# A new step order, key features on GpSimd, and wide products over all heads in an attention and FFN kernel on one core

## The chip, the cores and the metric

The kernel runs on one NeuronCore of a Trainium2 chip. The metric is the device time of one execution in microseconds, from the first to the last instruction with what lies around them; the median of three runs is given. Five engines work side by side, each through its own queue in order: TensorE (PE in the profile, its weight loads PEld), VectorE (DVE), ScalarE (ACT), GpSimd (POOL) and SyncE (SP), which issues most of the DMAs. They wait for each other by semaphores alone.

## The reference

Two blocks follow each other. The first is an attention without softmax: queries and keys are sketched to 8 + 8 numbers, whose outer product is a feature vector of 64.

```
def phi(x):                                  # q, k, v: (4, 4, 1088, 32); S1, S2: (8, 32)
    a = np.einsum('rd,bhsd->bhsr', S1, x)
    b = np.einsum('rd,bhsd->bhsr', S2, x)
    return np.einsum('bhsi,bhsj->bhsij', a, b).reshape(*x.shape[:-1], r * r)
q_p, k_p = (phi(q), phi(k))
kv = np.einsum('bhsf,bhsd->bhfd', k_p, v)
z = np.sum(k_p, axis=2)
num = np.einsum('bhsf,bhfd->bhsd', q_p, kv)
den = np.einsum('bhsf,bhf->bhs', q_p, z)[..., None] + 1e-06
attn = num / den
```

Its output, reshaped to 4352 rows of 128, goes through a multiplicative FFN:

```
a = x @ w1; b = x @ w2                       # 128 x 1024 each
h = a * b @ w3                               # 1024 x 1024
return h @ w_out                             # 1024 x 128
```

S1, S2 and the four FFN matrices are float64 and reach the core as raw 64-bit words.

## The kernel before

**Steps and order.** The kernel is a dictionary of small named steps, each a Python function that issues a few instructions. A string, ORDER, names all of them once; the steps are run in that order, and every engine's instructions are chained in it (lines 1514 to 1527). So ORDER is the queue of every engine at once, written out by hand or by a planner, and an instruction that waits holds up everything behind it on its own engine. Three more tables go with it: SLOTS gives each tile its buffer (`b` are the 8 PSUM banks, `x` three large buffers that k, v and q share, `raw` three for weight words), POOL names the steps that run on GpSimd instead of VectorE, ACTS those on ScalarE. `on(name)` looks a step up there.

**Steps by their names.**

- `s.*` prepares the sketches S1 and S2 from their words and spreads them into block tables (`s.blk`, `s.blkh`, `s.KS`, `s.AR`, `s.RC`), and their products for the denominator (`s.P*`).
- `k0` to `k3` are the keys of a batch: `load`, `max`, `g`, `lead` and `rest` split k into two parts; `gram` forms k's Gram matrix on PE; `Gm` to `Nr` turn it, in small VectorE steps with a few products between them (`T0`, `T1`, `N0`, `N1`), into a vector for the denominator; `tr`, `kT`, `ab`, `abc` or `abt` make the sketches of k, `kp` their outer products (the features), `kv` the product of features and v. `kr0`, `kr1` do the last 64 rows of two batches each. `kz`, `kq` are the transposed results that the queries are multiplied with.
- `q0` and `q1` are the two halves of batch 0's first 1024 queries, `q2` and `q3` those of batch 1, `q4` and `q6` the 1024 of batches 2 and 3 ("wide"), `qr` the last 64 rows of all four batches. `tr`, `max`, `l2`, `l1`, `rm` split them; `A*` and `C*` are their products with the sketches (L957, L1278, L1287); `sm` to `sc` put leading and remaining parts together; `al`, `p01`, `p2`, `p12`, `dn`, `de`, `rc` give the denominator and its reciprocal; `phi` is the outer product of features (L1128, L1382), `pt`/`pc` or `pT` its transposition, `x` the product with kz or kq (L1188, L1401), `xT` the copy into the FFN's input.
- `w0` to `w10` load and convert the weights: `c` and `m` on ScalarE, `j` on VectorE, `a0`, `a1` on GpSimd (L438). `f0` to `f7` multiply w3 and w_out into one matrix, w3o.
- `g0` to `g7` are the FFN for 512 rows each, `gr` for the last 256: for each of 8 chunks `a` and `b` on PE (L1441, L1451), `c` the copy of a to SBUF on ScalarE (L1446), `m` the product a times b on VectorE (L1457), `o` the product with w3o (L1464, L1471), then `oT` and `st` for the output.
- `warm` steps are products of zeros whose result nobody reads (L221).

Every float32 product on PE appears as two matmul rows in the trace. In `q_part` the first rows, q0, are of kind "A", the branch `if cut:`, with one multiply `xs`, one set of transposes `xt` and one copy `xT` for all 512 columns. In `q_wide` the last products `x` run in one or two parts `u`, with the row strip t outside and the heads h inside, and `A0` adds onto what the bank's start by `C0` left.

Of the kernel before, what the change touches and what calls it, by code (L numbers as in the profile page):

```python
# [61 lines left out]
c.zeros c.mask c.ident warm17 s.four k0.zero k0.loadr warm0 k0.load0 k0.load1 k0.max0 k0.max1 k0.g k0.lead0 s.load  # L62
k0.rest0 s.words warm3 k0.tr0 warm19 warm1 k0.gram0 k0.gram1 k0.lead1 k1.zero warm4 warm14 k0.tr1 s.pair s.low s.lead
s.sum s.rest s.T s.tc s.P q0.load k0.rest1 s.zero s.R k0.kT1 k0.gram2 q0.tr k0.gram3 k1.load q1.tr k1.loadr kr0.load
s.c q0.max k0.gram4 w1.load s.blk k1.max q0.l2 s.Pc k0.kT0 kr0.tr k0.ab1 k0.ab0 k0.Gm s.Pm s.blkh k0.Gt k1.g k0.Ga
q0.l1 q1.max k0.T0 k0.abc1 k0.Gb k0.T1 q1.l2 warm2 k0.kp1 warm21 warm7 k1.tr1 kr0.kT k0.abc0 k1.lead0 k0.Ta warm18
q0.A0 q1.l1 warm13 k0.kp0 warm28 k0.Tb kr0.ab kr0.abc k1.tr0 q0.rm s.Pp v0.zero k0.Ts k0.N0 k1.kT0 q0.C0 k1.rest0
v0.load q0.sma k0.N1 q0.sta k0.kv0 kr0.kp k0.kv3 v0.loadr k0.kv1 k0.kv2 k0.kvr k1.gram0 k1.gram1 k0.Na s.KS q0.sha
k0.Nr q0.C0t q0.sla k0.kvc k0.kvm warm5 warm12 q0.sca k0.Nf k0.Nb k1.kT1 k0.kzt k0.Nh k2.zero kr1.load kr1.tr q0.al
q0.phi0 q1.rm w0.load q0.A1 warm11 warm24 q1.A0 warm23 k0.kz kr1.kT kr1.ab warm16 k0.kqt warm22 warm6 k0.Nl q0.smy  # L70
q1.sm w1.c q0.sty k2.loadr q1.st q1.sh w0.c q0.pt0 warm10 q0.C1 q0.pc0 q0.shy k1.gram2 k1.gram3 q0.phi1 k1.gram4
q0.pt1 q0.C1t q0.pc1 w0.m q0.x0 q0.x1 q0.sly q0.p01 q0.scy q0.p2 q0.p12 q0.dn k1.Gm q0.de q0.rc w2.load q1.load q1.C0
w0.j q0.xs w0.a0 q1.sl k1.Gt q0.xt q1.scy q1.sca k1.Ga q1.p01 q1.al q0.xT q1.p2 q1.p12 k1.ab warm9 k1.abt q3.tr q1.dn
g0.3a q1.de w0.a1 w1.m w1.j g0.0a w1.a0 g0.2a q1.rc q1.bs q2.tr q1.phi g0.1a g0.2b g0.3c w2.m g0.3b w2.c k0.kq g0.0c
g0.4a k2.load k2.max q1.pt1 kr1.abc q2.max g0.4c g0.1c g0.3m q3.max q1.pt0 q1.pc0 q0.restT g0.6a g0.0b k2.g k1.Gb
k2.lead0 q1.pc1 w3.load k1.T0 q1.x k1.T1 k2.rest0 w2.j k1.Ta q2.l2 q1.xT k2.gram0 q1.restT k2.gram1 k2.gram2 k1.Tb
k1.Ts k2.gram3 k2.gram4 k1.N0 s.AR k1.N1 warm15 g0.0m k1.Na k1.Nb w4.load g0.2c q2.l1 w1.a1 g0.2m q2.load g0.4b g1.3a
k2.Gm g1.6a g0.6c w3.c k1.Nr g0.1b w4.m w3.j k2.Gt q2.rm g1.3c k2.Ga g1.5a g1.1a g1.6c w3.m k3.zero k2.Gb g0.1m g0.4m
s.RC g1.5c g1.1c q2.C0 q2.A0 q2.C1 k2.T0 k2.T1 v1.zero w2.a0 warm26 q3.l2 w4.c k3.loadr w3.a1 w3.a0 q2.At w2.a1 q2.Ct
q2.sm q2.st g1.5b q2.sh w4.j g1.1b g1.2b g1.0b g1.2a g0.6b g0.7b f0.t g1.2c g1.1m k2.Ta q2.sl w4.a0 q2.sc g1.5m f0.m  # L80
g1.4a g1.3b v1.loadr g0.6m w4.a1 g1.0a q2.p01 q2.al q2.p2 q2.p12 k2.Tb k1.kp0 k1.kp1 q3.l1 q4.tr g1.2m f1.t g1.4c
g1.0c g0.7a g0.5a f1.m q4.max g1.0m w5.load q2.dn w6.load w6.c q2.de v1.load k1.kv0 k1.kv2 k1.kv3 k1.kv1 k1.kvr q2.rc
w6.j q3.rm f0.o g0.7c g0.5c k1.kvc f1.o q3.C0 q3.A0 q3.C1 w6.m w9.load kh2.load warm20 k2.Ts g1.3m g0.0o g1.7b q2.bs
g0.7m k1.kqt g1.6b q3.At w9.m k1.kq w5.c g0.1o w7.load q2.phi0 w5.m q3.sm q3.Ct q2.pT0 g1.6m k2.N0 k2.N1 q3.st k2.Na
q2.x0 k2.Nb k2.kT1 g1.7a g0.5b w5.j w6.a1 w6.a0 q3.sh q2.xT0 g2.1a g1.7c w9.c g1.7m f3.t g0.5m w5.a1 v2.zero w5.a0
g2.6a q2.restT w9.j q3.sl q3.sc g2.0a w8.load g2.7a q4.l2 g1.4b f3.m g2.0c g2.1c w7.c w7.m f2.t k2.kT0 g1.4m q3.al
g2.3a g2.6b w9.a1 k2.Nr w9.a0 g2.0b f6.t f6.m q3.p01 q3.p2 w7.j q3.p12 g2.0m q3.dn f2.m q4.l1 f3.o w8.m g2.6c q3.de
g2.6m q4.rm k2.ab w8.c g2.7c f6.o g2.3c q4.C0 q4.A0 w8.j w7.a0 k2.abt w8.a1 q4.C1 warm8 f2.o g2.2a g0.2o g2.5a q4.Ct
g2.4a g2.7b w8.a0 w7.a1 g2.2c g1.0o f5.t q4.At k3.load kh3.load w10.load q3.rc q3.bs g2.4c g0.6o g1.1o q3.phi0 f5.m
f5.o w10.m g2.5c w10.c f4.t k3.max g2.7m k3.kT1 q3.pT0 f4.m g1.6o g1.3o q3.x0 f4.o q3.xT0 q4.sm g1.4o k3.g q4.st g0.3o  # L90
g0.5o q3.load g0.4o g3.1a g2.1b k2.kp0 kr1.kp k3.lead0 q4.sh v2.load q4.sl q4.sc w10.j g3.1c w10.a1 q4.al g1.5o q4.p01
w10.a0 f7.t f7.m g2.2b q4.p2 g2.5b q4.p12 q4.dn q4.de v2.loadr g2.1m q6.tr k2.kp1 q4.rc k3.kT0 k3.rest0 g3.6a g3.6b
g1.2o g3.6c f7.o g3.3a g0.7o g1.7o k2.kv0 k2.kv3 g2.5m g2.2m g1.oT k2.kv1 k3.ab k3.gram0 k3.gram1 k3.gram2 k2.kv2
k2.kvr k3.gram3 k3.gram4 q4.bs k2.kvc g3.3c warm27 g3.2a g3.2c q6.max k3.Gm g3.6m k3.Gt k3.Ga q3.restT g3.2b qr.max
v3.zero g2.4b g3.3b g3.0a q4.phi0 k3.Gb g0.oT g0.st v3.load k3.abt g3.4a q6.l2 k3.kp0 q4.phi1 q6.l1 g3.4c g3.4b q6.rm
g2.4m g2.3b q4.pT0 g3.3m q4.pT1 g3.0b g3.7a g2.0o k2.kqt g2.4o g3.7c k2.kq qr.l2 g3.2m g3.0c g2.6o g2.5o g2.3m g3.0m
k3.kp1 k3.T0 k3.T1 k3.Ta k3.Tb k3.Ts q4.x0 q4.x1 k3.N0 k3.N1 k3.kv0 k3.kv1 k3.kv3 v3.loadr k3.kv2 k3.kvr q4.xT0 q4.xT1
k3.Na k3.Nr g3.4m k3.Nb g3.5a q6.C0 q6.A0 q6.C1 k3.kvc k3.kqt k3.kq qr.l1 g3.5c g5.6a q6.Ct g3.7b q6.At q6.sm q6.st
q6.sh g5.0a g5.4a g5.4c g5.0c g5.2a g5.1a g2.3o q6.sl q6.sc q6.al q6.p01 q6.p2 q6.p12 q6.dn q6.de q6.rc q6.bs g5.5a
g2.2o g4.7a g5.5c g5.6c g5.1c g5.2c g5.7a g5.3a g3.1b g2.1o g5.3b g2.7o g3.0o g3.4o g5.7c q6.phi0 g5.3c q6.phi1 g3.1m  # L100
q6.pT0 g5.3m g2.oT q6.pT1 g3.3o q6.x0 q6.x1 g3.5b q6.xT0 q6.xT1 g3.1o g6.3a g6.1a g4.7c g5.6b g4.5a g6.3c g5.6m g4.5c
qr.rm g3.5m g3.7m g6.4a g3.6o g6.5a g5.1b g7.4a g6.5c g6.1c g6.4c g7.4c qr.C0 qr.A0 qr.C1 qr.Ct qr.At g4.0a g4.2a
g5.5b qr.sm g3.2o g5.0b g6.1b g4.4a qr.st qr.sh qr.sl qr.sc g4.0c g4.4c qr.al g6.1m qr.p01 qr.p2 qr.p12 qr.dn qr.de
qr.rc qr.bs qr.phi0 g7.0a g5.1m g5.2b g5.7b g4.2c g5.7m g5.5m g6.5b g5.4b g6.5m g4.6a g5.4m g7.6a g7.5a g5.2m g7.0b
g7.5c g7.6c g4.6c g7.0c g3.5o g6.2b g4.1a g4.0b g3.7o g3.oT g4.2b g6.2a g4.1b g4.1c g6.2c g4.2m g4.0m g7.3a g5.0m
g5.0o g7.2a g6.7b g7.5b g5.1o g7.5m g6.2m g7.0m g5.2o g6.6a g6.6b g6.7a g6.6c g7.3c g4.1m g6.0a g6.7c g6.0c g7.2c
# [15 lines left out]
def make_steps(ctx, tc, q, k, v, S1, S2, moe_w1, moe_w2, moe_w3, moe_w_out, out):  # L122
# [93 lines left out]
    def warm(name, times, tag="out"):  # L216
        @step(name)
        def _():
            t = ps(tag, [128, 256], "idle_ps")
            for _ in range(times):  # L220
                pe.matmul(t, zeros, bview(zeros, [[0, 2], [1, 128]]), start=True, stop=True)  # L221
# [1336 lines left out]
```

## Time and profile before

| | us |
|---|---|
| median of 3 runs | 256.75 (256.54 to 256.82) |
| span of the profiled execution | 254.9 |
| PE busy, matmul | 246.9 |
| DVE busy | 165.9 |
| ACT busy | 93.0 |
| POOL busy | 71.3 |
| FFN products a and b (L1441, L1451), busy | 132.4 |
| FFN products o (L1464), busy | 61.0 |
| products of zeros (L221), busy | 13.0 |

The span runs from the first to the last instruction of the profiled execution; the runs' times include some work around it. Busy times of pipelined matmuls overlap, so the rows of PE are not to be added up. The page cuts the span into 40 slices of 6.4 us, and each digit there is a busy share in tenths. The granted TensorE clock is 0.999 on average. 22.0 MB are moved, nearly all in the first 100 us.

### The profile page before, as it was taken

The page shows a single profiled execution, that of the slowest core. Times are in us where ns is not written, and L with a number is a line of the kernel's source. Part 1 is how long each engine was busy: PE and PEld are TensorE (multiplying, and loading weights), DVE is VectorE, ACT ScalarE, POOL GpSimd, SP SyncE. Part 2 cuts the span into 40 slices and gives each one's busy share as a digit, 9 for nine tenths or more (in the row PEclk, how much of TensorE's full clock was granted, in tenths as well). Part 3 has the DMA queues.
Part 4 walks back from the last instruction along what each step waited for, and adds up shares of the span by engine and source line. Part 5 has one row for each costly group of instructions (what it writes and reads, how often), then busy time and mean ns, then how long its engine had stood idle before and what let it go on. Part 6 is the DMA issues. An engine that isn't in the chain of part 4 may idle for free.

```text
span 254.9 us, 5984 instructions
## 1 busy us (share of the span) xinstructions
PE 246.9 (97%) x2503; PEld 138.4 (54%) x2503; DVE 165.9 (65%) x364; ACT 93.0 (37%) x175; POOL 71.3 (28%) x97
## 2 busy tenths in 40 slices
PE   8899999999999999999799999999999999999994
PEld 6788845456545747455346444444444444555454
DVE  3999899899989899893695876235443124433240
ACT  2776467925488414211432350441220400121000
POOL 3433383467645472801480041001000000000000
PEclk9999999999999999999999999999999999999999
DMA  6887994899296592000140002000000000430133
GB/s 189 252 220 188 272 238 122 179 240 237 79 214 137 144 242 40 3 0 3 22 109 3 3 0 42 3 0 1 3 0 0 0 0 3 69 55 0 24 58 62
DMA packets 32074, 22.01 MB, mean 86 GB/s; under 512 B 21296, under 2 KB 26672, under 8 KB 32048
## 3 DMA queue, kind: packets, MB, share of 16 engines
q1 hardware_dynamic: 31360, 21.05, 35.1%
q10 hardware_dynamic: 688, 0.59, 0.8%
q8 instruction: 19, 0.31, 0.5%
q14 instruction: 7, 0.06, 0.1%
HBM read 19.40 MB, written 2.23 MB: 85 GB/s over the span
## 4 chain that ended last, share of the span: by engine, by line
PE 89%; DVE 5%; DMA 2%; issue 1%; SPq 1%; POOL 1%; DVEq 0%
PE a_ps L1441 23%; PE b_ps L1451 23%; PE ps_o L1464 22%; PE ps_w3o L471 6%; PE ps_g L597 2%; PE ps_x L1401 2%; PE ps_ac L1287 2%; DMA kr<-in_k_dram 2%; PE ps_or L1471 1%; PE ps_kv L707 1%; DVE kp L615 1%; PE ps_ab L665 1%; PE ps_xt L1188 1%; DVE q L947 1%; POOL kk L589 1%
## 5 line engine op out<-in xcount | busy, mean ns | idle before, releaser
L1446 ACT COPY ffa<-a_ps 128x512 f32<-128x512 f32 (+1 forms) x72 | 38.7, 566 | 93.8 <-PE a_ps L1441 89.4
L1457 DVE TENSOR_TENSOR ab<-ffa,b_ps 128x512 f32<-128x512 f32 (+1 forms) x72 | 44.7, 647 | 41.2 <-PE b_ps L1451 40.2
L1451 PE MATMUL b_ps<-xT,w 128*128 128x512 f32 (+1 forms) x144 | 66.6, 570 | 0.1
L1441 PE MATMUL a_ps<-xT,w 128*128 128x512 f32 (+1 forms) x144 | 65.8, 571 | 0.0
L1464 PE MATMUL ps_o<-ab,w3o 128*128 128x512 f32 x128 | 61.0, 594 | 0.0
L1451 PEld LDWEIGHTS b_ps<-xT,w 128*128 128x128 f32 x144 | 26.8, 190 | 30.5 <-issue 24.9
L1441 PEld LDWEIGHTS a_ps<-xT,w 128*128 128x128 f32 x144 | 26.6, 190 | 27.6 <-issue 22.2
L1464 PEld LDWEIGHTS ps_o<-ab,w3o 128*128 128x128 f32 x128 | 23.8, 190 | 26.3 <-issue 25.3
L438 POOL TENSOR_TENSOR w3c<-w3c,cv_m 128x512 int32<-128x512 int32 x16 | 20.6, 1306 | 18.2 <-DVE w3c L432 15.0
L1480 DVE STREAM_TRANSPOSE oT<-ps_o 128x512 f32<-128x512 f32 x8 | 5.7, 714 | 18.5 <-PE ps_o L1464 18.5
L471 PEld LDWEIGHTS ps_w3o<-wo,w3T 128*128 128x128 f32 x128 | 15.3, 192 | 2.9 <-issue 1.9
L1382 POOL TENSOR_TENSOR ph<-s_al,s_bs 128x1024 f32<-128x1024 f32 (+1 forms) x6 | 12.7, 2120 | 12.4 <-DVE s_bs L1372 9.4
L471 PE MATMUL ps_w3o<-wo,w3T 128*128 128x128 f32 x128 | 15.3, 275 | 0.0
L221 PE MATMUL idle_ps<-zeros 128*128 128x256 bf16 x72 | 13.0, 313 | 1.0 <-DVE zeros L193 1.0
L229 ACT ACTIVATE cv_c<-raw 128x1024 f32<-128x1024 f32 x11 | 12.7, 1162 | 0.0
L419 ACT ACTIVATE cv_m<-raw 128x1024 int32<-128x1024 uint32 x11 | 12.6, 1157 | 0.0
L1412 ACT COPY xT<-ps_x 128x128 f32<-128x128 f32 (+2 forms) x20 | 4.6, 323 | 19.5 <-PE ps_x L1401 19.5
L615 POOL TENSOR_TENSOR kp<-kabt 128x1024 f32<-128x1024 f32 x5 | 9.7, 1946 | 3.4 <-DVE kabt L683 3.4
L465 DVE STREAM_TRANSPOSE w3T<-w3c 128x1024 f32<-128x1024 f32 x8 | 9.9, 1233 | 1.2 <-POOL w3c L438 1.2
L1304 DVE STREAM_TRANSPOSE ay_C<-ps_ac 128x128 f32<-128x128 f32 (+2 forms) x20 | 5.3, 321 | 6.7 <-PE ps_ac L1287 6.7
L597 PE MATMUL ps_g<-k,kk 128*32 128x32 f32 x288 | 7.7, 194 | 1.7 <-issue 1.7
L221 PEld LDWEIGHTS <-zeros 128*128 128x128 bf16 x72 | 7.4, 112 | 3.6 <-DVE zeros L193 1.0
(240 smaller groups left out, 284.7 us busy)
## 6 DMA issues: line engine op xcount, KB each, us to landing
raw<-in_moe_w_dram SPq DMA_DIRECT2D x32, 256.0 KB, 6.0
qh<-in_q_dram SPq DMA_DIRECT2D x4, 544.0 KB, 5.2
out_dram<-oT SPq DMA_DIRECT2D x33, 64.0 KB, 2.0
raw<-in_moe_w_dram SPq DMA_DIRECT2D x4, 512.0 KB, 5.7
k<-in_k_dram SPq DMA_DIRECT2D x3, 512.0 KB, 7.0
v<-in_v_dram SPq DMA_DIRECT2D x2, 512.0 KB
raw<-in_moe_w_out_dram SPq DMA_DIRECT2D x4, 256.0 KB, 6.0
kh<-in_k_dram SPq DMA_DIRECT2D x8, 128.0 KB, 2.5
```

The source lines that it names most:

```text
L221: pe.matmul(t, zeros, bview(zeros, [[0, 2], [1, 128]]), start=True, stop=True)
L229: act.activation(dst, hi.bitcast(F32), ACT.Prelu, scale=2.0 ** -112, alpha=-2.0 ** 32)
L419: act.mul(x["m"], words(0).bitcast(U32), 2.0 ** -29)
L438: pool.tensor_tensor(d, d, x["m"][:, i * 512:(i + 1) * 512], ALU.add)
L471: pe.matmul(t["o"], w3T[ko][:, c], wo[:, c], start=c == 0, stop=c == NC - 1)
L597: pe.matmul(o[h * D:(h + 1) * D], lhs, rhs, start=start, stop=stop, skip_group_check=True)
L1382: on(nm(f"phi{u}")).tensor_mul(x, bview(s["al"][:, u * g], [[r, g], [1, r], [0, r]]), bview(s["bs"][:, u * g], [[r, g], [0, r], [1, r]]))
L1441: pe.matmul(x["a"][:, :w], w_of(0, c), xT[g][:, c0:c0 + w], start=True, stop=True)
L1446: act.copy(x["s"][:, :w], x["a"][:, :w])
L1451: pe.matmul(x["b"][:, :w], w_of(1, c), xT[g][:, c0:c0 + w], start=True, stop=True)
L1457: dve.tensor_mul(ab_sb[g, c][:, c0:c0 + w], x["s"][:, :w], x["b"][:, :w])
L1464: pe.matmul(o_ps[g], w3o[:, c], ab_sb[g, c], start=c == 0, stop=c == NC - 1)
```

## The change

- ORDER and SLOTS are new in all parts. q0.restT comes early and v0 takes q0's buffer instead of k0's. The ACT step c.act comes first instead of near the end.
- WARM has 4 steps of 21 products of 512 columns instead of 28 of 72 products of 256.
- POOL: the features of the first keys (k0.kp0, k0.kp1), k0.rest0, k1.rest0, k2.rest0, k2.lead0, k3.lead0, k2.kp1, q0.p01, s.sum, s.KS, and several sc, sl, bs, p01 steps move to GpSimd; s.blk, s.blkh, k2.kp0, k3.kp0, k3.kp1, q2.p12, q4.phi0, q6.phi1 and q6.al move to VectorE. q0.phi0 and q0.phi1 change places.
- q0's end is cut into halves of 256 columns: x, xs, xt and xT each come twice.
- The x step of `q_wide` is one step over all heads, the head outside and the row strip inside; A0 starts its own columns of the bank and stands ahead of C0.
- `kp` in the kv steps is looked up when it is used. w.j is always on VectorE.

ORDER's first lines in the new kernel, up to the first FFN products:

```
c.zeros k0.zero k0.load0 c.ident s.four c.mask s.zero k0.loadr k0.load1 s.load c.act k0.max0 k0.max1 k0.g k0.lead0
warm0 warm1 k0.tr1 q0.load k0.kT1 s.words s.pair q0.restT s.low k0.tr0 s.lead k1.zero k1.load k0.lead1 k0.rest0 k0.kT0
q0.tr s.sum q1.tr s.rest warm2 k0.gram0 k0.gram1 s.T q0.max s.P s.tc s.R s.c k1.tr1 s.Pm kr1.load k1.loadr kr0.load
kr0.tr s.blk kr1.tr k0.ab0 k1.max q1.max k0.rest1 s.blkh s.Pc s.Pp v0.zero v0.load q0.l2 kr0.kT k0.abc0 q0.l1 k0.gram2
k0.gram3 k0.gram4 k0.Gm q1.l2 kr0.ab q0.rm k0.ab1 q0.A0 k1.tr0 k0.Gt k1.g k0.Ga k0.Gb k0.T0 k0.kp0 k0.Ta kr0.abc
k0.kv0 k0.abc1 q0.C0 k1.lead0 q0.sma k0.T1 k0.Tb warm3 k0.N0 k0.Ts k0.N1 k0.kp1 q1.l1 v0.loadr q0.sta k0.Na q0.sha
w1.load k0.Nb k0.kv3 k0.kv1 kr1.kT k0.Nf kr0.kp k0.kv2 k0.Nl q1.rm k0.Nh q0.C0t k0.kvr k0.kvm q0.C1 q0.A1 w0.load w1.m
q0.sla q0.smy q0.sca q0.al q0.sty k1.rest0 q0.shy q0.sly v1.zero q0.phi0 k0.kzt k0.kvc q0.C1t q0.phi1 q0.scy k2.zero
q1.C0 q0.p01 q0.p2 w1.c w1.j k0.kz k1.kT0 k1.gram0 q0.p12 q0.dn k1.gram1 k1.gram2 q0.pt0 q0.pc0 q0.pt1 q0.pc1 k0.kqt
q1.A0 kr1.ab q1.sm q0.de q0.x0 q0.x1 k1.gram3 w0.c k0.kq k1.gram4 k1.kT1 q0.rc q0.xs0 q0.xs1 k1.Gm k1.Gt k1.Ga q0.xt0
s.KS q0.xT0 q0.xt1 k1.Gb q0.xT1 w0.m w1.a0 w1.a1 k1.ab k1.T0 k1.T1 g0.6a q1.st w0.j w4.load w0.a0 g0.5a kh2.load g0.6c
g0.5c g0.7a q1.sh q1.sl q1.sca q1.p01 q1.scy q1.al kr1.abc k1.Ta k1.Tb k1.Ts g0.1a g0.2a g0.0a g0.4a g0.4c q1.p2
q1.p12 q1.dn q1.de q1.rc q1.bs s.RC v1.load q1.load k2.loadr q2.tr k2.load g0.6b w0.a1 g0.0b v1.loadr k1.abt q1.phi
k0.Nr q2.max k2.max g0.2b k2.kT0 k2.kT1 g0.0c g0.2c q1.pt0 q1.pt1 q2.l2 g0.3a q2.l1 g0.7c w2.load q1.pc0 q1.pc1 g0.3c
g0.6m g0.0m q2.rm k1.N0 k1.N1 k2.g s.AR k1.kp0 k1.kp1 k1.Na k1.Nr k1.Nb q1.x q1.xT k2.lead0 g0.1c k2.ab q2.A0 q2.C0
```

and at its end:

```
g6.6o g6.4o g6.1o g6.3o gr.4m gr.1b gr.1m g6.7o gr.6o0 gr.5o0 gr.6o1 gr.5o1 gr.1o0 gr.1o1 gr.4o1 gr.3o1 gr.4o0 gr.3o0
gr.2c gr.2m gr.2o0 g6.oT g6.st gr.7m gr.2o1 gr.7o0 gr.oT0 gr.st0 gr.7o1 gr.oT1 gr.st1
```

The rest of the diff, cut to its core:

```diff
-WARM = [16, 10, 6] + [4] * 2 + [2] * 8 + [1] * 16
+WARM = [11, 2, 7, 1]
...
 POOL = set("""
-    k0.Nh k0.rest1 k1.kp0 k1.kp1 k2.kp0 k3.kp0 k3.kp1 k3.rest0 q0.p2 q0.phi1 q1.p12 q1.p2 q1.phi q2.al
-    q2.p12 q2.p2 q2.phi0 q3.al q3.phi0 q4.phi0 q4.phi1 q6.al q6.phi1 qr.p2 qr.phi0 s.Pp s.blk s.blkh
-    s.rest
+    k0.Nh k0.Nr k0.kp0 k0.kp1 k0.rest0 k0.rest1 k1.kp0 k1.kp1 k1.rest0 k2.Nr k2.kp1 k2.lead0 k2.rest0
+    k3.Ts k3.lead0 k3.rest0 q0.p01 q0.p2 q0.phi0 q1.al q1.p12 q1.p2 q1.phi q2.al q2.bs q2.p01 q2.p2
+    q2.phi0 q2.sc q3.al q3.bs q3.p12 q3.p2 q3.phi0 q3.sc q3.sl q4.al q4.bs q4.p2 q4.phi1 q4.sc q4.sl
+    q6.p12 q6.p2 q6.phi0 q6.sc qr.al qr.p01 qr.p12 qr.phi0 s.KS s.Pp s.rest s.sum
 """.split())
...
-            t = ps(tag, [128, 256], "idle_ps")
+            t = ps(tag, [128, 512], "idle_ps")
             for _ in range(times):
-                pe.matmul(t, zeros, bview(zeros, [[0, 2], [1, 128]]), start=True, stop=True)
+                pe.matmul(t, zeros, bview(zeros, [[0, 4], [1, 128]]), start=True, stop=True)
...
-                    if u == 0:
-                        s["x"] = ps("h", [128, nj, H * D], "ps_xt")
-                    o = s["x"]
-                    for j in range(2 * u, 2 * u + 2):
+                    s["x", u] = o = ps("h", [128, hj, H * D], "ps_xt")
+                    for j in range(hj):
...
+                @step(nm(f"xs{u}"))
+                def _(u=u):
...
+                    dve.tensor_mul(s["xs"][:, hj * u:hj * (u + 1)].rearrange("p j (h d) -> p (j h) d", d=D),
+                                   s["x", u].rearrange("p j (h d) -> p (j h) d", d=D),
+                                   bview(s["rc"][:, hj * H * u:], [[1, hj * H], [0, D]]))
+
+                @step(nm(f"xt{u}"))
+                def _(u=u):
+                    s["xp", u] = t = ps("t", [128, 256], "ps_xs")
+                    for j in range(hj):
+                        pe.transpose(cols(t, j), s["xs"][:, hj * u + j], ident)
+
+                @step(nm(f"xT{u}"))
+                def _(u=u):
+                    act.copy(x_dst()[:, 256 * u:256 * (u + 1)], s["xp", u])
...
-                              start=False, stop=True, tile_position=(p * 64, t * 32), skip_group_check=True)
+                              start=True, stop=True, tile_position=(p * 64, t * 32), skip_group_check=True)
...
-            @step(nm(f"x{u}"))
-            def _(u=u):
-                if u == 0:
-                    s["x"] = [ps(t, [128, 512], "ps_x") for t in BANKS]
-                for i in range(2):
+        @step(nm("x"))
+        def _():
+            s["x"] = [ps(t, [128, 512], "ps_x") for t in BANKS]
+            for i in range(2):
+                for h in range(H):
                     for t in range(4):
-                        for h in range(u * H // parts, (u + 1) * H // parts):
...
```

More of the change, by code (lines that the diff above doesn't have):

```diff
@@ L61 @@
 ORDER = """
[L62 to L106, printed above, removed]
```

125 lines of the change are left out of this document (69 added, 56 removed).

## The prediction

> **What bounds the kernel now.** The page's first two parts come first.
>
> ```profile
> span 254.9 us, 5984 instructions
> PE 246.9 (97%) x2503; PEld 138.4 (54%) x2503; DVE 165.9 (65%) x364; ACT 93.0 (37%) x175; POOL 71.3 (28%) x97
> ...
> PE   8899999999999999999799999999999999999994
> ...
> DVE  3999899899989899893695876235443124433240
> ...
> POOL 3433383467645472801480041001000000000000
> ```
>
> PE is full almost throughout, but two stages hide in that. The table of busy times by stretch gives DVE 25.3 of the first 31 us, 73.8 of 31 to 110 and 66.8 of the last 145: until about 110 us DVE is nearly as full as PE and decides whether PE's inputs come in time; after that PE alone counts. The chain of waits shows where the head ends:
>
> ```profile
> 21.70 0.69 DVE ph L1128
> 22.39 1.48 DVE q L947
> ...
> 30.29 0.60 PE ps_ab L665 x32
> 30.89 0.33 PE idle_ps L221 x2
> 31.21 3.52 PE a_ps L1441 x8
> ```
>
> The first FFN product is issued at 31.1. From there PE has no long gap but one, in the same chain:
>
> ```profile
> 120.32 0.42 PE ps_g L597 x19
> 120.74 1.68 issue
> 122.42 0.38 PE ps_g L597 x8
> ```
>
> So the time is the head's length, plus what PE must still do, plus PE's later gaps, plus a tail of 3.5 us behind the last product at 251.4. The timelines of DVE and POOL show what makes the head long:
>
> ```profile
> 16.68 0.67 DVE L947 SCALAR_TENSOR_TENSOR q<-q,qT 128x512 f32<-128x512 bf16 x1
> 21.81 1.51 POOL L1128 TENSOR_TENSOR ph<-s_al,s_bs 128x512 f32<-128x512 f32 x1 [1.36 <-DVE s_al L1090]
> 22.31 1.56 DVE L947 SCALAR_TENSOR_TENSOR q<-q,qT 128x512 f32<-128x512 bf16 x1
> ...
> 27.98 0.17 DVE L1114 SCALAR_TENSOR_TENSOR s_rc<-s_d 128x16 f32<-128x16 f32 x1
> ...
> 32.25 1.27 POOL L438 TENSOR_TENSOR w<-w,cv_m 128x512 int32<-128x512 int32 x1
> 32.78 0.78 DVE L1114 SCALAR_TENSOR_TENSOR s_rc<-s_d 128x16 f32<-128x16 f32 x1
> ```
>
> The same DVE instruction takes 0.67 alone and 1.56 when POOL is in a two-input operation: it ends 0.55 after POOL's end (23.32). L1114 takes 0.17 and 0.78, ending with POOL's 33.53. All DVE instructions with two SBUF inputs that begin inside a POOL operation of over 1 us do this; those with a PSUM input (the FFN multiply L1457) do not. It works the other way too: POOL's L778 takes 1.42 beside a DVE subtract and 0.63 elsewhere. I call this the lock.
>
> The Trainium skill, GPSIMD Engine Reference, section 1, says that GpSimd shares its SBUF interfaces with VectorE and contends with DVE instructions that have two SBUF inputs. The trace agrees (0.67 against 1.56). The page's section 4.1 puts two-input elementwise work at about twice the time on GpSimd; here it is 1.95 against 1.2, and neither hides the work from DVE.
>
> **The change, part by part.** All against the profiled execution, 254.9; the median of the runs, 256.75, lies 1.85 above it and I add that at the end.
>
> *Head, work alone.* DVE loses the first k subtract (0.69), both kp products (1.24, 1.21), the next batch's subtract (1.34), q0's p01 (0.40), the sketch sum (0.21) and KS (0.18): 5.3. It gains s.blk and s.blkh (about 0.5 by DVE's small rows) and q0.restT (0.23). Walking the new queues without the lock: 11 + 2 wide fillers end at 5.8 (256 columns take 213 ns until 5.02, 110 ns after, so 512 take twice that); tr1 0.44, its copy 0.57, s.words 0.4 end at 7.4; q0 lands at 8.0 as before, and q0.restT, s.lead, q0.tr and q1.tr fill DVE to 10.1. The moved v0.load takes q0's buffer and waits for q1.tr, with w1, w0 and w4 behind it on SP: w1 (1.05 MB behind 0.52) at 235 GB/s lands near 17, ahead of its use near 19, so it costs nothing; without that cover, each microsecond late is one on w1.a0. Gram, T0 (15.3), N1 (17.1), Nl (18.7; 24.0 now), the last sc (23.0; 26.6 now), rc (25.8; 28.4 now). The end in halves has two multiplies of about 0.36 (half of 0.68), transposes behind each, and a last copy of about 0.35 instead of 0.59: 1.4 from rc to the last copy's end, 1.95 here since x1's products end after rc; now it is 2.5, with a w.j of 0.63 between. First FFN product: 28.0, against 31.1: **-3.1**, the best end. c.act goes first on ACT, so I expect the table load (1.28, now at 4.98) in idle time; if it stays ahead of s.words, s.lead comes 0.5 later, inside this range.
>
> *Head, with the lock.* POOL now holds kp0 (1.95) from about 13.0, kp1 (1.95) from 15.1, kr0.kp (0.63), and, after Nh, k1.rest0 (2.62, the 128x1152 row). DVE's queue in that stretch is s.blkh, Gm, q0.rm, Gt, k1.g, Ga. s.blkh waits for kp0 to 14.9, q0.rm for kp1 to 17.6, k1.g for kr0.kp to 18.3; behind them stand Ga, T0, N0. Na then ends at 21.4 instead of 17.8, k1.rest0 starts at 21.8, and Nf, Nl, q1.rm and C0t wait behind it to 24.4. From there rc is 8.0 away (q1.rm, C0t and sixteen rows of 0.2 to 0.45 to p12 and dn; phi0 holds shy for 1.4, p01 holds phi1 for 0.4, w1.a0 holds de for 1.3), and the last copy 1.4 more. First product: 33.9, **+2.8**, the worst end. Every overlapping pair in the trace shows the lock, so I stand near this end, but a pair dodged by a few tenths saves a whole POOL operation: 33.0, **+1.9**.
>
> *k1's T products* (0.31 at 40.3 and 41.5) now lie in the head: **-0.3**.
>
> *x over all heads.* Consecutive products now use four row strips under one column strip, as L1287 does already. The chain has:
>
> ```profile
> 49.09 0.43 PE ps_ac L1287 x32
> ...
> 87.34 0.73 PE ps_ac L1287 x32
> ...
> 101.44 1.00 PE ps_x L1401 x56
> ...
> 157.88 1.72 PE ps_x L1401 x59
> ```
>
> 64 of them at L1287's pace are 0.86 (128 columns) and about 1.4 (256): two parts save 0.13, two 0.32, the rest rows 0.13: **-1.1** (0 if the order is no matter, -1.6 at best). A ahead of C alone moves eight products of 0.2: 0.
>
> *Fillers.* Seven in the main stage, 0.7 on PE; some stand in gaps: **-0.5** (0 to -0.7).
>
> *Gap at 120.7.* 1.68 in which PE waits for nothing that the profile shows (k3.rest0 had ended at 107.9), and 0.4 around it, among k3's many small products. The new order has the same products with others between; nothing says whether the gap comes again, so half: **-1.0** (0 to -2.1).
>
> *31 to 110 again.* Each step of the two written orders priced with its row and added up by engine, the queues from the first FFN product to the fold f7.m (the last or the last but one) now need 86 us of PE, 80 of DVE and 61 of POOL; before, 75, 69 and 43. DVE's share of PE is as it was (0.93 and 0.92), but POOL's goes from 0.57 to 0.71 and its pieces are longer (k2.rest0 2.6, kp and phi 1.95, against the 1.27 of L438 that fill most of it now). Before, the lock cost DVE 5.0 us in this stage (eight stretched rows: 0.60, 0.25, 0.72, 0.38, 0.63, 0.14, 1.06, 1.24). Times 1.25 for POOL's share and about 1.5 for its pieces it is 9.5, some 4.5 more on a DVE with 0 to 5 us of slack. Beside it, q2's products wait for q1.load, which waits for k1's buffer and lands near 32.6, then k2.max, q2.rm, k1.Na: 2.6 of PE stall by that walk, as against 1 now at this place. **+3.0** (0 to +6).
>
> *Tail.* Behind the last product the same copy and store; g6's four stores (1.95) start 2.2 before PE's end, clear of the last: 0.
>
> Sum: +1.9 - 0.3 - 1.1 - 0.5 - 1.0 + 3.0 = +2.0, a span of 256.9; with 1.85, **258.7**. Its own range, from the head at +0.5 to +2.8 and the main stage at +1 to +6, is 255.4 to 262.6.
>
> **Rivals.** (1) *Faster: the lock is dodged.* The queues drift so that POOL's long pieces fall beside DVE's PSUM work. For it: only eight rows in 79 us were stretched. Against: in the head both queues are packed. It decides from where the first FFN product comes before 30. Start -2.3, main stage +1.0: -2.3 - 0.3 - 1.1 - 0.5 - 1.0 + 1.0 = -4.2, 252.6. (2) *The clock falls.* 72 fillers become 21 (7.8 us of issue to 4.5); if PE's head gets sparse the clock drops to half, at which an FFN pass takes 0.86 for 0.43, until it rises again; the rise took 4.0 us (1.0 to 5.0), so 2 to 4 us on top: 261.7. Against: the granted clock stayed at 1.00 in 19 to 28, where PE did small work. (3) *Cancelled.* A lock that costs less: head +0.9, main stage +2.0, so +0.9 - 0.3 - 1.1 - 0.5 - 1.0 + 2.0 = 0.0: 256.75. For it: one dodged pair in the head is enough. (4) *The x order doesn't do what it says.* The wide parts stay at 1.72 and the others at 1.00: +1.1 on mine, 259.8. Against: L1287 has that order and that pace.
>
> The Trainium skill, TensorE: Matmul & The Clock Gate, Part 1, says that the clock halves after an idle window of about 3.4 us. By that, only a head without PE work that long would bring rival 2; no run here shows one yet.
>
> **Numbers.** Likeliest 0.46, (1) 0.34, (2) 0.09, (3) 0.07, (4) 0.04. About 0.2% is what a measurement of this kernel tells from no change. Faster is (1) and a sliver of the likeliest's low end, 0.36; same 0.07; slower 0.57. The range goes from just under rival 1's 252.6 to the likeliest's upper end: 251.5 to 262.5.
>
> **What would show it.** Head: the first a_ps after 32, with q0.rm, k1.g, Nf and de stretched to the ends of kp1, kr0.kp, k1.rest0 and w1.a0; before 30 and unstretched, I am wrong and rival 1 holds. x: 0.9 and 1.4 a part. Main stage: more stretched two-input DVE rows and PE gaps between 35 and 50. Clock: first FFN passes at 0.86. A total under 254 would mean the moves to POOL do free DVE.

## The result, and the profile after

The changed kernel takes 273.24 us (median, 272.67 to 273.62), beside 256.64 for the kernel before on the same chip: 1.0652 times as long, with a 95% interval of 1.063 to 1.0674. The forecast was 258.7, the range ended at 262.5. The sign was right, the size was not: 16.6 us instead of 2.

The first two parts of the page of the changed kernel, to be laid beside those of before:

```profile
span 271.1 us, 5909 instructions
...
PE 253.4 (93%) x2452; PEld 139.3 (51%) x2452; DVE 169.9 (63%) x340; ACT 93.1 (34%) x176; POOL 99.6 (37%) x122
...
PE   8966999479999799999999999999999999999994
...
DVE  3898579986699979997873244976123622343122
...
POOL 4765728857637947557750000141000200000000
PEclk9995599959999999999999999999999999999999
```

POOL took 28 us more, as the moves meant, yet DVE is no less busy. PE has two weak places, about 14 to 27 and 47 to 61 (its digits 6 6 and 4 7), and in both the granted clock falls to half: from 19.9 to 33.6 and from 54.0 to 60.9. The chain of waits goes through stretched DVE rows in the head, and in the main stage, where it named no wait of DVE before, it now has some too:

```profile
13.44 1.85 DVE Rh L328
15.40 0.60 DVE q L945
16.09 1.73 DVE k_g L575
...
21.59 2.65 DVE RS L871 x2
24.27 1.13 PE ps_cy L955 x16
...
49.60 1.08 DVE q L1263
51.20 3.65 DVE RC L168
```

Rh, k_g, RS and RC are the lock again: L575 (k_g) works on two numbers a partition. The table of busy times, cut at the clock's own steps of 3.41 us (start and end, length, busy time of PE, PEld, DVE, ACT and POOL, then the granted clock, DMA share and GB/s):

```profile
13.07:16.48 3.41, 2.78 (x83) 2.38 (x72) 3.41 (x6) 1.79 (x5) 2.83 (x2) 1.00 0.84 202
16.48:19.90 3.42, 1.55 (x45) 1.24 (x45) 2.88 (x10) 1.96 (x2) 1.93 (x2) 1.00 0.96 311
19.90:23.31 3.41, 2.16 (x72) 1.87 (x72) 3.06 (x10) 2.42 (x6) 2.12 (x2) 0.50 1.06 294
23.31:26.72 3.41, 2.45 (x27) 2.10 (x27) 3.04 (x10) 2.49 (x5) 1.03 (x3) 0.50 1.05 268
26.72:30.14 3.42, 3.42 (x57) 3.25 (x60) 3.28 (x6) 0.00 (x0) 2.45 (x4) 0.50 0.87 205
30.14:33.55 3.41, 3.41 (x75) 3.28 (x67) 0.73 (x2) 0.79 (x2) 2.92 (x4) 0.50 0.06 17
33.55:36.97 3.42, 3.42 (x75) 3.31 (x73) 1.89 (x7) 2.17 (x4) 0.00 (x0) 1.00 0.00 0
...
50.63:54.04 3.41, 0.19 (x8) 0.00 (x0) 3.34 (x6) 1.73 (x3) 3.12 (x1) 1.00 0.08 20
54.04:57.45 3.41, 1.60 (x72) 0.87 (x72) 3.02 (x10) 0.00 (x0) 3.33 (x2) 0.50 0.00 0
```

A stretch in which PE is busy for 1.55 or 0.19 is followed by one at half clock. From 24.27, where the wait for RS ends, to the first FFN product PE's timeline has no wait over 0.15: that part of the head is as long as PE's own work, and up to 33.55 this runs at half clock. The second weak place comes from one instruction; the timelines of POOL, DVE and PE in that order:

```profile
50.92 4.25 POOL L175 TENSOR_SCALAR kk<-k,k_g 128x1152 f32<-128x1152 f32 x1 [0.79 <-PE ps_ab L663]
51.20 3.64 DVE L168 SCALAR_TENSOR_TENSOR RC<-N_g,N_t 128x8 f32<-128x8 f32 x1
54.88 0.17 DVE L879 TENSOR_TENSOR AR<-RC,mask2n 128x16 bf16<-128x16 f32 x1
55.10 0.31 PE L1276 MATMUL ps_ac<-q,AR 64*32 64x128 bf16 x8 [4.28 <-DVE AR L879]
```

k2.lead0, on POOL now, takes 4.25 where DVE needs 0.88 for the same shape; a DVE instruction of 8 columns (L168, two SBUF inputs) waits for it, and q2's A products wait for that. The first FFN product starts at 38.02 instead of 31.06. So 7.0 of the span's 16.2 us are lost in the head, and 9.2 behind it, most of them before 62 (behind 62 PE stands idle for 6.9 us, before the change for 5.5).

### The profile page after: what moved, and what is told of

Read it like the earlier page. It is cut to its first block, busy times and chain, and to the rows that moved or that the text cites. A ratio compares the mean times of both kernels' runs of the same rounds, so it can differ in the third digit from the quotient of the medians.

```text
span 271.1 us, 5909 instructions
## 1 busy us (share of the span) xinstructions
PE 253.4 (93%) x2452; PEld 139.3 (51%) x2452; DVE 169.9 (63%) x340; ACT 93.1 (34%) x176; POOL 99.6 (37%) x122
## 3 DMA queue, kind: packets, MB, share of 16 engines
q1 hardware_dynamic: 31360, 21.05, 33.9%
## 4 chain that ended last, share of the span: by engine, by line
PE 72%; DVE 19%; issue 3%; ACT 2%; DMA 2%; SPq 0%; POOL 0%; DVEq 0%; ACTq 0%; POOLq 0%
PE ps_o L1461 20%; PE b_ps L1448 16%; PE a_ps L1438 16%; PE ps_w3o L469 3%; PE ps_g L595 3%; PE idle_ps L219 3%; PE ps_ac L1285 2%; DMA raw<-in_moe_w_dram 2%; DVE ab L1454 2%; DVE RC L168 1%; PE ps_or L1468 1%; PE ps_x L1398 1%; DVE w3c L430 1%; DVE RS L871 1%; PE ps_kv L705 1%
## 5 line engine op out<-in xcount | busy, mean ns | idle before, releaser
L1448 PE MATMUL b_ps<-xT,w 128*128 128x512 f32 (+1 forms) x144 | 67.6, 580 | 0.4 <-DVE ay_C L1302 0.4
L1438 PE MATMUL a_ps<-xT,w 128*128 128x512 f32 (+1 forms) x144 | 67.8, 580 | 0.0
L1448 PEld LDWEIGHTS b_ps<-xT,w 128*128 128x128 f32 x144 | 26.6, 192 | 29.7 <-issue 23.1
L1332 POOL TENSOR_TENSOR s_hl<-s_hl,ay_C 128x256 f32<-128x256 f32 (+1 forms) x4 | 4.9, 1234 | 33.1 <-DVE s_hl L1328 33.0
L1380 POOL TENSOR_TENSOR ph<-s_al,s_bs 128x1024 f32<-128x1024 f32 (+1 forms) x5 | 9.9, 1984 | 7.4 <-DVE s_bs L1370 7.2
L587 POOL TENSOR_TENSOR kk<-k,kk 128x1152 f32<-128x1152 f32 (+2 forms) x5 | 11.1, 2215 | 3.3 <-DVE kk L175 3.1
L1351 POOL TENSOR_TENSOR s_pr<-s_pr 128x128 f32<-128x128 f32 (+2 forms) x3 | 1.5, 501 | 23.9 <-DVE s_pr L1347 22.6
L1388 DVE STREAM_TRANSPOSE pT<-ph 128x1024 f32<-128x1024 f32 (+1 forms) x7 | 8.1, 1158 | 2.7 <-POOL ph L1380 2.7
L175 POOL TENSOR_SCALAR kk<-k,k_g 128x1152 f32<-128x1152 f32 x2 | 8.5, 4252 | 2.3 <-PE a_ps L1438 1.5
```

Source lines behind the costliest of these rows:

```text
L587: on(f"k{b}.rest{u}").tensor_sub(chunks(kk[b][:, 1], u), chunks(k_sb[b], u), chunks(kk[b][:, 0], u))
L1380: on(nm(f"phi{u}")).tensor_mul(x, bview(s["al"][:, u * g], [[r, g], [1, r], [0, r]]), bview(s["bs"][:, u * g], [[r, g], [0, r], [1, r]]))
L1438: pe.matmul(x["a"][:, :w], w_of(0, c), xT[g][:, c0:c0 + w], start=True, stop=True)
L1448: pe.matmul(x["b"][:, :w], w_of(1, c), xT[g][:, c0:c0 + w], start=True, stop=True)
```

## The experiments

All times below are medians, and every ratio is to the kernel before on the same chip. Not all runs were on one chip, so where two kernels are compared the ratios count more than the times.

**Which part of POOL's new work costs.** First on the changed kernel: three key steps back on DVE, then the two leads.

```diff
-k0.kp0 k0.kp1 k1.rest0     (e2: out of POOL)
-k2.lead0 k3.lead0          (e3: out of POOL)
```

> The changed kernel with k0.kp0, k0.kp1 and k1.rest0 back on VectorE, nothing else. Theory (POOL's long two-input operations hold DVE by the lock): DVE gets 3.8 us of work (1.24, 1.21, 1.34) and loses waits of 1.1 at k_g, 1.7 at Rh, 2.6 at RS and some small ones, T0's products come at 16 to 17 instead of 18.1, the hole of PE in front of Nf and Nl shrinks from 2.4 to under 1, the first FFN product comes at 34 to 36.5, the time falls by 2 to 4. Rival (the new order of DVE's queue is late by itself, wherever these three run): the first FFN product stays at 37.5 or later, the time at 273 or above.

271.24 us, 1.0599 (1.0572 to 1.0625), first FFN product at 35.89; T0's products came at 15.4. The first FFN product is 2.1 earlier, so the theory holds; the gain, 2.0 by the medians and 1.4 by the ratios, is at or under the low end of what was expected. The granted clock falls here too, at half from 19.4 to 29.7, with these steps off POOL. Within q0's C1 PE now stands 1.52 with no wait for anything that the profile shows ("issue"); this comes back below.

> The changed kernel with k2.lead0 and k3.lead0 back on VectorE (two tensor_scalar of 128x1152 by a pointer, 4.25 us each on POOL, 0.8 on DVE). Theory: k1.Na's subtract at 51.2 takes 0.3 instead of 3.65, PE's stall of 4.5 in front of q2's A products goes down to under 1, and the clock does not fall a second time at 54 to 60: time 5 to 7 lower, about 267. Rival (k1.N and q1's end are late for other reasons, and DVE pays the leads): something else of DVE stands in front of A, and the time falls by less than 2.

268.97 us, 1.0505 (1.047 to 1.0539): 4.3 less by the medians, 3.8 by the ratios. L168 takes 0.17 and the hole in front of A is 0.81. The gain is under the 5 expected; the clock still fell at 53.9, behind a stretch with PE busy for half.

The same two edits on the order of before:

```diff
+k0.kp0 k0.kp1 k1.rest0     (b1: into POOL)
+k2.lead0 k3.lead0          (b3: into POOL)
```

> The kernel before with k0.kp0, k0.kp1 and k1.rest0 on GpSimd, nothing else: the prediction's head term on the old order. Theory (the lock): DVE loses 3.8 us of work but waits in two-input instructions for POOL's 1.95, 1.95 and 2.65; first FFN product at 32 to 34 instead of 31.1, time at 257.5 to 260. Rival (the moves free DVE, the lock is dodged): first FFN product at 29 to 30.5, time at 254.5 to 256. The whole new list of GpSimd steps on this order cost 17 us; this says how much of it is in the head.

258.71 us, 1.0102 (1.0049 to 1.0155), first FFN product at 33.55. The first FFN product is 2.5 later although DVE has 3.8 us less work: this is the lock, shown by an edit. It is not the same sum as the prediction's +2.8, which also holds what the new order was to win (33.9 with the lock, 28.0 without). The granted clock stayed at 1.00 from 4.4 to the last product. Its timeline of POOL and DVE:

```profile
13.45 3.87 POOL L615 TENSOR_TENSOR kp<-kab 128x1024 f32<-128x1024 f32 x2 [2.01 <-ACT kab L646]
14.61 0.83 DVE L170 SCALAR_TENSOR_TENSOR T_p<-T_g,T_t 32x32 f32<-32x32 f32 x1
15.79 2.07 DVE L947 SCALAR_TENSOR_TENSOR q<-q,qT 128x512 f32<-128x512 bf16 x1
...
19.20 2.63 POOL L589 TENSOR_TENSOR kk<-k,kk 128x1152 f32<-128x1152 f32 x1
20.38 1.49 DVE L170 SCALAR_TENSOR_TENSOR RC<-N_g,N_t 128x8 f32<-128x8 f32 x1
```

> The kernel before with k2.lead0 and k3.lead0 on GpSimd, nothing else. Theory: each takes 4.25 us there instead of 0.8 and k2's and k3's Gram products wait for the part behind it: holes of PE of 3 to 4.5 us at some 45 to 50 and of 1 to 3 near 120, time at 260 to 265. Rival (this order has slack behind its leads, and the 17 us of the whole list come from elsewhere): holes under 1, time at 256 to 258.

263.51 us, 1.0264 (1.0222 to 1.0307): some 7 for two instructions. In DVE's queue the subtraction of the leading part from k (k2.rest0) just waits, PE's Gram products wait for that, and the clock is at half from 46.4 to 49.8:

```profile
38.93 4.25 POOL L177 TENSOR_SCALAR kk<-k,k_g 128x1152 f32<-128x1152 f32 x1 [1.15 <-PE ps_ph L1166]
43.21 2.43 DVE L589 TENSOR_TENSOR kk<-k,kk 128x1152 f32<-128x1152 f32 x1 [4.12 <-POOL kk L177]
45.69 0.34 PE L597 MATMUL ps_g<-kk 128*32 128x64 f32 x8 [3.63 <-DVE kk L589]
```

The Trainium skill, GPSIMD Engine Reference, section 4.1, calls one-input work on GpSimd "roughly line-rate". Here a tensor_scalar with two operations by a pointer takes 4.25 (up to 6.25 in b2) against 0.87 to 0.88 on DVE for the same shape; the measurement decides.

**The order and the list by halves.** In e5 the new order got the old list of POOL steps, in b2 the old order the new list.

> The changed kernel with its list of GpSimd steps as the kernel before has it (its own order, buffers, fillers, halves and x order stay). Theory (what lies on POOL is the cause): DVE has about 12 us more work of its own but no long lock in the head, the first FFN product comes at 34 to 36, the stall at 50 is gone, the time at 262 to 266. Rival (the new order alone): the time stays at 270 or above with the first FFN product behind 37.

> The kernel before with the changed kernel's list of GpSimd steps, as far as its steps look it up (k0.kp0, k0.kp1, the rests, the leads, k2.kp1 and so on go to POOL, s.blk, s.blkh, k2.kp0, k3.kp0, k3.kp1, q2.p12 and others to VectorE; sc, sl, bs and p01 are fixed on VectorE in it); order, fillers and products as before. Theory (the moves to POOL cost by themselves): the lock stretches DVE in the head and k2.lead0 takes 4.2 us on POOL: first FFN product at 32 to 35, time at 259 to 266. Rival (only the new order is at fault): first FFN product at 30.5 to 31.5, time at 255 to 257.5.

e5: 277.9 us, 1.0833 (1.079 to 1.0875), first FFN product at 39.90. b2: 273.52 us, 1.0668 (1.0641 to 1.0694), at 34.09. The old order with the old list is at 256.6, the new with the new at 273.2. Each half alone costs 17 and 21 us, both together 16.6: the halves do not add, and putting the whole list back was no repair. In e5 the figures are the rival's, and b2 is slower than either side said. My theory, that the list is the cause, falls in this form; what holds of it are e2, e3, b1 and b3. Why e5 is the slowest of all is not explained here.

**The clock.** bw cuts the fillers of the kernel before to 37 narrow products ahead of 11 us; e1 adds wide ones to the changed kernel, e7 a few float32 ones to e3.

```diff
-WARM = [16, 10, 6] + [4] * 2 + [2] * 8 + [1] * 16
+WARM = [16, 10, 0, 4, 4, 0, 0, 0, 0, 0, 0, 0, 0, 0, 1, 0, 0, 1, 0, 1, 0, 0, 0, 0, 0, 0, 0, 0, 0]
...
+pe.matmul(t, ident, bview(ident, [[0, 4], [1, 128]]), start=True, stop=True)
```

> The kernel before with its fillers cut to the 37 narrow products ahead of 11 us (the changed kernel has 42 of that width there); all later ones are left out. Theory (the clock falls for the holes that waits make, and this kernel has no long ones): granted clock at 0.95 or more from 12 to 31, first FFN product at 31 to 31.5, time 256 to 257.5. Rival (fewer fillers alone bring the fall): clock at half somewhere between 15 and 32, first FFN product at 33 to 35, time 258.5 to 261.

256.83 us, 1.0022 (0.9988 to 1.0055). The clock and the head are the rival's, the time is the theory's: PE had a hole of 2.56 up to 22.1 and the clock was at half from 22.5 to 25.9, the first FFN product came at 33.13, 2.1 late, and the time hardly changed, with the 1.68 hole at 120.7 gone. From the table of bw, the stretch with the hole and the one behind it:

```profile
19.08:22.49 3.41, 0.85 (x66) 0.69 (x57) 3.17 (x16) 0.11 (x1) 0.45 (x3) 1.00 0.18 71
22.49:25.90 3.41, 3.38 (x67) 3.09 (x57) 3.13 (x8) 3.21 (x8) 1.31 (x2) 0.50 0.43 108
```

So fewer fillers alone bring the fall in the old order (bw), and the lock alone, with all 72 fillers, does not (b1). All the traces divide that way: ahead of the first FFN product the clock falls in each of the twelve kernels with fewer fillers and in none of the six that kept the 72. Eleven of the twelve have the new order too, and no run puts the 72 into that order.

> The changed kernel with 21 wide fillers more in the holes of PE's head: 8 before k0's T products (hole at 15.5 to 18.1), 3 in place of 1 ahead of N, 10 after the last kv product (hole at 21.9 to 24.3). Theory (the holes that the lock makes let the clock fall, and half a clock is 4 us of the head): the granted clock stays at 1.00 from 15 to 38, the stretched DVE rows stay as they are (k_g 1.8, Rh 1.9, RS 2.7), the first FFN product comes at 34 instead of 38.0, the time falls by 3 to 4.5 to about 269.5; the stall at 50 stays. Rival (the head waits for DVE anyway, the clock is only a sign of it): the clock rises but the first FFN product stays within 1 us of 38, and the time at 272.5 to 273.5.

273.3 us, 1.0682 (1.0657 to 1.0706). The clock stayed up to 25.9 instead of 19.9, but the first FFN product came at 38.26: the rival's figures. The clock was at half from 25.9 to 32.7 all the same, among PE's last rows ahead of that product. The ten fillers behind the last kv product did not run in a row:

```profile
21.06 1.25 PE L219 MATMUL idle_ps<-zeros 128*128 128x512 bf16 x5
24.52 1.25 PE L219 MATMUL idle_ps<-zeros 128*128 128x512 bf16 x5 [2.21 <-issue]
25.71 0.52 PE L955 MATMUL ps_cy<-q,RS 128*32 128x128 f32 x8
```

Products of zeros wait for nobody. The hole stands behind 348 of the program's matmuls, in bw behind 347, in e2 346, in e3 347: the same place, whatever the work there. The trace has packets of 16 KB on a queue of kind "instruction", one at 21.78 in e1 and at 19.69 in bw, and PE goes on 2.4 to 2.7 us later. It does not say whose they are. That they are PE's instructions is read from the times: all 17 holes over 0.4 us that PE's timelines put down to "issue", in all runs, end 2.2 to 3.0 us behind the start of one. The hole at 120.7 of the kernel before is of the same kind: a packet at 119.91, the next product at 122.42.

> The changed kernel with k2.lead0 and k3.lead0 on VectorE (as in e3_leads_on_dve) and six products of a float32 identity with itself that nobody reads, 512 columns each, in PE's holes: two ahead of k0.T0, two after the last kv product of k0, one ahead of q2's A products and one ahead of q2's C1. In e3 the clock fell at 19.7 after a stretch of 3.41 us in which PE was 0.45 busy, and at 53.9 after one of 0.50; these few products fill such a stretch to 0.7 or more and need 24 instructions of PE instead of the 42 of e1_fill. Theory (the clock falls where a stretch of 3.4 us is less than some 0.55 busy; this costs some 4 us in the head and 2.5 behind 54): the clock stays at 1.00 from 6 to the end, the first FFN product comes at 34.5 to 35.5 instead of 38.6, the time at 262 to 264 instead of 269. Rival (half a clock costs little, since DVE sets the pace of the head): the clock stays up, the first FFN product is still behind 37, and the time at 267 or above.

267.67 us, 1.0446 (1.0417 to 1.0475). The fall at 54 is gone; beside e3 that is 1.3 less, with intervals that just touch. The head is hardly better, 37.84, which is the rival's figure again; two such holes (0.84, 1.14) and one stretch at half clock (27.0 to 30.4) remain. So no edit here gives the price of half a clock in the head by itself.

The traces give an account of it. In all eleven kernels of the new order PE has the same 237 rows from q0.A1, just behind C1, to the first FFN product. They take 11.3 to 13.6 us, 3.4 to 9.3 of that at half clock. Less PE's waits and less half of the time at half clock, 8.5 to 9.1 is left in every one of them. By this estimate half a clock costs half of its length there: 4.1 of the 12.7 us of the changed kernel, which have 8.2 at half clock.

**Do the parts add?** e9 is the changed kernel with e2's and e3's edits and e7's two later fillers; e10 moves two more things in the head.

```diff
-k1.kT0 k1.gram0 q0.p12 q0.dn k1.gram1 k1.gram2 q0.pt0 ... kr1.ab q1.sm q0.de q0.x0 ... q0.xs1
+k1.kT0 q0.p12 q0.dn q0.pt0 ... kr1.ab k1.gram0 k1.gram1 k1.gram2 q0.de q0.x0 ... q0.xs1 q1.sm
```

> The changed kernel with k0.kp0, k0.kp1, k1.rest0, k2.lead0 and k3.lead0 on VectorE and two float32 fillers, one ahead of q2's A and one ahead of its C1 (no others added). If the parts add (2.0 from e2, 4.3 from e3, 1.3 to 2.4 from the clock behind 54 in e7): 264 to 265.5, no second fall of the clock, first FFN product at 35.5 to 36.5. If they are two sides of one wait: 266 to 268.

> e9 with two things moved in the written order: k1's first three Gram steps behind q0's phi transposes on PE (they stood ahead of them) and q1.sm behind q0's end on VectorE (it stood ahead of q0.de and waited 1.9 to 2.7 us for PE's q1.A0). Theory (the rest of the head's loss is work of the next part that the new order puts ahead of q0's end): phi's transposes start at 29 to 30, the reciprocal at 31 to 33 instead of 34.4, first FFN product 1.5 to 2.5 us earlier than in e9, time 1 to 2.5 lower. Rival (PE's clock and the loading of its instructions set that stretch, wherever the steps stand): first FFN product within 0.7 of e9's.

e9: 265.29 us, 1.0336 (1.0277 to 1.0395): the times add, 8 of the 16.6 us are found. The head missed what was expected: its first FFN product comes at 37.21, behind e2's 35.89. e10: 266.73 us, 1.042 (1.0363 to 1.0478), first FFN product at 37.95: about what its rival said, and moving these steps won nothing. Its hole in C1 is 0.97, but its clock is at half for 13.7 us where e9 has 10.2, so what the order alone is worth is not told.

**PE's instructions and the weights.** In e9 the hole within C1 is 2.88. The change had moved the loads of v0, w1, w0 and w4 into one row, issued from 10.3 to 17.5; the DMA share in e9 is 0.86 to 1.08 from 14.6 to 24.9. Two edits hold w0 and w4 back by a word that DVE writes first: e11 on e9, e12 on the changed kernel.

```diff
 raw[n] = sb("raw", [128, 1024], I64)
+if n in (0, 4):
+    dve.memset(raw[n].bitcast(I32)[:1, :1], 0)
```

> e9 with the loads of w0 and w4 (1 MB each, issued at 12.7 to 17.5 in one row behind v0 and w1) held back: VectorE writes one word of the buffer first, w0 behind q1.rm at about 22, w4 behind w0.j at about 38; nothing else. In e9 and e10 the DMA engines are full from 15 to 28, PE's second block of instructions (16 KB) starts to be fetched 3 to 5 us after PE has passed the 512th row, and PE stands 2.9 us at the 347th product for nothing but that. Theory (the moved weight loads make PE's own instructions late; with the hole the clock goes): the fetch starts within 1 us, the issue hole goes to under 0.7, the clock falls for two stretches of 3.4 us at most, first FFN product at 34 to 35.5 instead of 37.2, time at 262 to 264. Rival (the fetch is late by itself, whatever else is loaded): hole and time as in e9, 264.5 to 266.

> The changed kernel itself with w0 and w4 held back in the same way, nothing else. Theory: there the block's lateness lies behind the lock's hole at 21.9 to 24.3, so the gain is smaller than in e11: 0.5 to 1.5, time at 271.5 to 272.7. Rival of e11: no difference, 273.

In e9 PE passed the 512th row of its instructions (matmuls and weight loads counted) at 17.4 and the packet started at 22.09; in e11 17.41 and 17.84. PE's timeline at C1 and at the first FFN product, e9 first, then e11:

```profile
21.43 0.65 PE L965 MATMUL ps_cy<-qT,RS 128*32 128x128 f32 x5
24.95 0.64 PE L965 MATMUL ps_cy<-qT,RS 128*32 128x128 f32 x3 [2.88 <-issue]
37.21 1.12 PE L1448 MATMUL a_ps<-xT,w 128*128 128x512 f32 x2
```

```profile
21.63 0.68 PE L967 MATMUL ps_cy<-qT,RS 128*32 128x128 f32 x8
33.72 1.12 PE L1450 MATMUL a_ps<-xT,w 128*128 128x512 f32 x2
...
48.40 2.08 PE L1460 MATMUL b_ps<-xT,w 128*128 128x512 f32 x2 [6.45 <-DVE kabt L693]
```

The hole is gone and the first FFN product 3.5 earlier: the late packet was the weights' doing. The time is 270.78, 1.0578 (1.0542 to 1.0613), since the second batch's loads stand behind w4 on SP and a hole of 6.45 follows. e12: 276.91 us, 1.0811 (1.0773 to 1.0849), first FFN product at 37.72; with the lock's hole still over the same place, only 0.3 is won there, and the time, which was to fall, rises: PE stands 5.24 ahead of 51.2, at the same place as in e11.

e13 lets w4 go behind q0.dn, at 29.2 instead of 34.4:

> e11 with w4's load released behind q0.dn (at about 29) instead of behind w0.j (34.4 in e11); w0 as there. In e11 the fetch of PE's block came 0.4 after its row, the issue hole went and the first FFN product came at 33.7 instead of 37.2, but k2's and q1's loads, which stand behind w4 in SP's queue, came some 5 late and PE stood 6.4 in front of 48. Theory: the head stays at 33.7, that hole goes, time at e9's 265.3 minus 3.5: 261 to 263. Rival (the loads only move the hole from one place to another): 264.5 or above.

265.65 us, 1.0357 (1.0323 to 1.0391), with the first FFN product at 33.95. The rival holds. DVE's timeline shows the second limit:

```profile
41.74 0.71 DVE L1262 STREAM_TRANSPOSE qT<-qh 128x512 f32<-128x512 f32 x1 [1.69 <-DMA qh<-in_q_dram]
...
44.82 1.35 DVE L184 TENSOR_REDUCE k_m<-k 128x1 f32<-128x1152 f32 x1 [1.14 <-DMA k<-in_k_dram]
```

In e9 the same two start at 43.22 and 45.07 with no wait. The second batch's data are there no earlier, and q2's C1 starts at 53.4 in e9 and 54.0 in e13, where the filler in front of A also runs at half clock (2.07 for 1.13): in the new order PE meets q2's products after only 22 FFN rows, so what a faster head wins is given back there.

**x over all heads, and a better kernel.** bx puts that one edit on the kernel before. bz adds c.act early and k3's last two Gram steps, with Gm, Gt and Ga, behind g3.2b.

```diff
+for h in range(H):
     for t in range(4):
-        for h in range(u * H // parts, (u + 1) * H // parts):
...
-k2.kvr k3.gram3 k3.gram4 q4.bs ... q6.max k3.Gm g3.6m k3.Gt k3.Ga q3.restT g3.2b
+k2.kvr q4.bs ... q6.max g3.6m q3.restT g3.2b k3.gram3 k3.gram4 k3.Gm k3.Gt k3.Ga
```

> The kernel before with the wide parts' last products x over all heads, the head outside and the row strip inside, as in the changed kernel (where a part has two x steps, the second issues all); nothing else. From the changed kernel's rows: q4 1.5 and q6 1.43 instead of 1.72, q2, q3 and the rest unchanged at 1.0 and 0.78: -0.5 us, time at 256.0 to 256.3 beside 256.6. By the prediction's own term: 0.9 a part of 128 columns and 1.4 of 256, -1.1 us. If the order is no matter at all: no difference.

256.28 us, 1.0003 (0.9976 to 1.0029). In the trace q6's part goes from 1.72 to 1.43 and q4's shrinks alike, the narrow ones stay at 0.98 and 1.00. The 1.1 of the prediction lies outside the interval; whether it is 0.6 or nothing is not settled.

> The kernel before with x over all heads (as in bx), c.act early (ACT's table load of 1.28 at 1.7 instead of 4.98) and k3.gram3, gram4, Gm, Gt, Ga behind g3.2b, so that k3's small products do not come in one row of 208; nothing else. PE stands 1.68 at 120.7 in the kernel before while its block of instructions, fetched at 119.9, is not there. Theory: with FFN products of 0.43 between them the block has time to land, the hole goes to under 0.7; the head gains 0 to 0.8 from the table load: time 1 to 2 lower than before, 254.5 to 255.5. Rival (the hole moves to the next row of small products, the head is DVE's): 256 to 256.6.

255.35 us, 0.9966 (0.9946 to 0.9985): 0.8 faster than the kernel before, and the best of all here. The hole at 120.7 is gone; the longest that PE's timeline has from 116 to 128 is

```profile
120.44 1.12 PE L1449 MATMUL a_ps<-xT,w 128*128 128x512 f32 x2 [0.25 <-ACT kvc L743]
```

and the first FFN product is at 30.94 for 31.06, so hardly any of it comes from the head. What the x edit, which bz has too, adds to the hole's part is not told apart.

## Why the prediction was off

- **The lock in the head** was right in its mechanism and near in its size. T0's product came at 18.07; the chain of stretched rows was the one walked, but for k_g waiting for kp1 in q0.rm's place, and RS behind k1.rest0 ends at 24.24 where the walk had 24.4. By edits the moves cost 2.1 of the head (e2) and 2.5 (b1). That I took 1.9 instead of the walk's 2.8, for a dodged pair, is the smaller fault.
- **The step of the head that failed is the clock**, left out of the likeliest case. From 24.4 to the first product my walk had 9.5, in rows of DVE; it took 13.8, with PE at work throughout and at half clock up to 33.55. By the account above half a clock is 4.1 of that, and 38.0 less 4.1 is 33.9, the walk's own worst end. So the 6.95 for 1.9 is 0.9 of the lock and some 4.1 of the clock; the 4.1 is worked out from the traces and not shown by an edit.
- **Why rival 2 got 0.09:** the clock had stayed at 1.00 in 19 to 28 while PE did small work. But in the kernel before no stretch of 3.41 us from 8.6 to 29 has PE busy for under 2.79, with fillers in most of them; a wait of 2 us makes one of 1.55. Rival 2 named the condition that the runs bear out, the fillers: the clock falls in bw without the lock, stays up in b1 with it, and falls in e2 with these steps off POOL. That the lock and fewer fillers together would leave PE so little was not put together in the forecast.
- **The moved loads were costed at nothing**, with the argument that w1 lands ahead of its use. What I named as cover was the weights' own use; what became late was PE's instructions (e11: 3.5 us of the head once the lock is gone, 0.3 beside it in e12). In the changed kernel the late packet lies behind the lock's hole.
- **Main stage, +3.0 (0 to +6).** Behind the head the kernel lost 9.2 where all my terms together gave +0.1. The largest piece is k2.lead0, which I moved to POOL in the queue sums as if it were a short step; it is 4.25, its hole 4.28, with the clock's fall behind it (six FFN rows 4.32 instead of 2.58). e3 gives 4.3 for the two leads (3.8 by the ratios), the fillers of e7 another 1.3. My bound looked at the lock and at POOL's share, and missed a single instruction with a price that no row of the trace showed: DVE's row of 0.88 was a bound from below alone.
- **q2 waits for its loads** was in the walk, at 2.6. e13 shows it as a limit of its own, hidden under the others.
- **The gap at 120.7** did go; I called it half. Its cause, which I left open, is the loading of PE's instructions.
- **x over all heads** was sized at -1.1 and is 0.6 at most; the narrow parts kept their pace, as rival 4 had it for all. The fillers' -0.5 can't be read from bw, whose head is later and whose hole at 120.7 is gone.
- **Left open:** some 9 us of e9 against the kernel before. The head is 6.1 of it, and by the account above the hole (2.9) and half a clock (3.1) are nearly all of that; e13 takes 3.3 of the head away and the time does not follow. What the new order would take at full clock, and the rest behind the head, are not shown.
